# Attention with grouped queries on one core: another first ten microseconds, and one more shared chunk

## The chip, the cores and the metric

The kernel runs on one core of one Trainium2 chip. Its time is the device time of one execution in microseconds (us).

## The reference

```python
B, Hq, Hkv, Sq, Sk, D = 16, 32, 8, 288, 512, 128       # bf16
k = jnp.repeat(k, 4, axis=1); v = jnp.repeat(v, 4, axis=1)
scores = jnp.einsum("bhqd,bhkd->bhqk", q, k) * D ** -0.5
out = jnp.einsum("bhqk,bhkd->bhqd", softmax(scores), v)
```

There are 128 groups (16 x 8). A group has one K and one V of 512 rows and 4 x 288 = 1152 queries, that is nine tiles of 128.

## The kernel before

A group is three chunks of 1536 columns of scores, 384 chunks in all. TensorE computes the scores of chunk n into one of two halves of PSUM, then the values (twelve matmuls of 129 columns, the last column being the sum of the weights) of chunk n - 2. ScalarE takes the exponential of a chunk in one instruction. VectorE divides by the sums, GpSimd copies V beside its column of ones, SyncE issues the loads and stores.

```python
for n in range(NS):                  # TensorE, NS = 384
    op_s(n)                          # scores of chunk n
    if shared(n): op_sy(n)           # 120 columns of every sixth chunk go to VectorE's own exponential
    if n == 2: op_kt(1, range(NJ), 1)    # K of group 1: four transposes through PSUM
    if n >= LAG: op_pv(n - LAG)      # values, LAG = 2
```

K and the queries arrive transposed by the load, but for K of groups 0 and 1. Those come as they are, on ScalarE's queue, and TensorE transposes them. VectorE copies them out of PSUM.

```python
first = [op_q0(0), op_v(0, None, 0, 1),
         op_q(1), op_k(0, 2), op_v(0, None, 1, UG), op_q(2), op_q(3)]     # SyncE's first loads
...                                  # (lambdas left out), then, sorted by time:
sp.append((t + (2.0 if u >= NSLOT else 0.35), lambda u=u: op_v(u)))       # V of groups 4u to 4u+3
```

The first two chunks and the last go through ScalarE in three parts each, so that it can start after one matmul.

## Time and profile before

| | kernel before |
|---|---|
| time, median of the first 3 runs | 522.71 us (522.05 to 522.73) |
| span of the profiled execution | 520.0 us |
| TensorE, ScalarE, VectorE busy | 98%, 99%, 71% |
| six chunks in steady state | 7.98 us |
| first scores, first exponential | 4.41, 5.05 us |

The prediction shows the busy shares and the main groups. Two more lines of the page: the chain that ended last, by engine, and the group of the score matmuls (count, then busy time and mean ns, then idle time before them).

```profile
ACT 98%; DMA 1%; issue 1%; DVE 0%; PE 0%
...
L439 PE MATMUL ps_s<-qt_sb,kt_sb 128*128 128x512 bf16 (+2 forms) x1430 | 290.4, 320 | 5.0 <-DMA qt_sb<-in_q_dram 0.5
```

The weight loads of the same line are 1536, so 106 records of matmuls are missing from this trace: 98% for TensorE is an undercount, and the 5.0 us of idle time are mostly those holes.

### The profile page before, as it was taken

The page shows a single profiled execution, that of the slowest core. Times are in us where ns is not written, and L with a number is a line of the kernel's source. Part 1 is how long each engine was busy: PE and PEld are TensorE (multiplying, and loading weights), DVE is VectorE, ACT ScalarE, POOL GpSimd, SP SyncE. Part 2 cuts the span into 40 slices and gives each one's busy share as a digit, 9 for nine tenths or more (in the row PEclk, how much of TensorE's full clock was granted, in tenths as well). Part 3 has the DMA queues.
Part 4 walks back from the last instruction along what each step waited for, and adds up shares of the span by engine and source line. Part 5 has one row for each costly group of instructions (what it writes and reads, how often), then busy time and mean ns, then how long its engine had stood idle before and what let it go on. Part 6 is the DMA issues. An engine that isn't in the chain of part 4 may idle for free.

```text
span 520.0 us, 15243 instructions
## 1 busy us (share of the span) xinstructions
PE 510.3 (98%) x6118; PEld 394.6 (76%) x6224; DVE 369.6 (71%) x1315; ACT 513.3 (99%) x393; POOL 79.8 (15%) x135
## 2 busy tenths in 40 slices
PE   8999999999999999999999999999999999999997
PEld 5777777777777777777777777777777777777776
DVE  2767767777777677676776776767767767677776
ACT  7999999999999999999999999999999999999997
POOL 2111111111111111111111111111111111111110
PEclk9999999999999999999999999999999999999999
DMA  9999999999999998999999989999998989998212
GB/s 186 237 218 230 267 194 248 225 213 210 219 233 256 208 245 201 235 248 240 215 241 209 209 225 220 241 185 209 229 240 232 227 194 201 192 234 198 86 69 93
DMA packets 253078, 110.06 MB, mean 212 GB/s; under 512 B 219728, under 2 KB 236752, under 8 KB 253008
## 3 DMA queue, kind: packets, MB, share of 16 engines
q1 hardware_dynamic: 252720, 108.82, 97.7%
q8 instruction: 49, 0.80, 0.7%
q10 hardware_dynamic: 288, 0.26, 0.2%
q14 instruction: 21, 0.17, 0.2%
HBM read 17.04 MB, written 37.75 MB: 105 GB/s over the span
## 4 chain that ended last, share of the span: by engine, by line
ACT 98%; DMA 1%; issue 1%; DVE 0%; PE 0%
ACT pt_sb L516 97%; DMA qt_sb<-in_q_dram 1%; ACT pt_sb L511 1%; PE ps_s L439 0%; DVE o_sb L585 0%; DVE o_sb L595 0%; PE ps_s L479 0%; DVE rl_sb L575 0%; PE ps_o L669 0%; DVE bad_sb L621 0%; DVE flag_i L734 0%; DVE bad_sb L618 0%
## 5 line engine op out<-in xcount | busy, mean ns | idle before, releaser
L516 ACT ACTIVATE pt_sb<-ps_s 128x1536 bf16<-128x1536 f32 (+2 forms) x384 | 508.8, 1441 | 0.0
L479 PE MATMUL ps_o<-v_sb,pt_sb 128*128 128x129 bf16 x4584 | 322.3, 220 | 1.1
L479 PEld LDWEIGHTS ps_o<-v_sb,pt_sb 128*128 128x128 bf16 x4584 | 282.8, 98 | 49.7 <-DVE o_sb L585 14.1
L439 PE MATMUL ps_s<-qt_sb,kt_sb 128*128 128x512 bf16 (+2 forms) x1430 | 290.4, 320 | 5.0 <-DMA qt_sb<-in_q_dram 0.5
L585 DVE TENSOR_TENSOR o_sb<-ps_o,rl_sb 128x384 bf16<-128x384 f32 x382 | 211.9, 555 | 9.3 <-DVE rl_sb L575 0.5
L439 PEld LDWEIGHTS ps_s<-qt_sb,kt_sb 128*128 128x128 bf16 x1536 | 123.9, 98 | 62.3 <-issue 1.1
L575 DVE RECIPROCAL rl_sb<-ps_o 128x3 f32<-128x3 f32 x382 | 68.1, 178 | 125.5 <-PE ps_o L479 124.0
L568 POOL COPY v_sb<-vd_sb 128x512 bf16<-128x512 bf16 x128 | 78.8, 616 | 429.1 <-PE ps_o L479 408.9
L549 DVE SCALAR_TENSOR_TENSOR u_sb<-u_sb,m_sb 128x120 f32<-128x120 f32 x126 | 35.6, 283 | 2.2
L556 DVE SCALAR_TENSOR_TENSOR pt_sb<-u_sb,e_sb 128x120 bf16<-128x120 f32 x63 | 17.8, 283 | 2.2
L549 DVE SCALAR_TENSOR_TENSOR u_sb<-m_sb 128x120 f32<-128x120 f32 x63 | 17.4, 277 | 0.0
L527 DVE TENSOR_SCALAR y_sb<-ps_o 128x120 f32<-128x120 f32 x63 | 15.9, 253 | 0.0
L540 DVE TENSOR_SCALAR m_sb<-t_sb 128x120 int32<-128x120 int32 x63 | 14.1, 223 | 2.2
L540 DVE TENSOR_SCALAR e_sb<-t_sb 128x120 int32<-128x120 int32 x63 | 13.6, 216 | 0.0
L450 PE MATMUL ps_o<-qt_sb,kt_sb 128*128 128x120 bf16 x63 | 13.6, 216 | 0.0
L533 DVE TENSOR_SCALAR t_sb<-y_sb 128x120 int32<-128x120 f32 x63 | 13.4, 213 | 0.0
L450 PEld LDWEIGHTS ps_o<-qt_sb,kt_sb 128*128 128x128 bf16 x63 | 6.2, 98 | 7.4
L511 ACT ACTIVATE pt_sb<-ps_s 128x512 bf16<-128x512 f32 x6 | 3.3, 616 | 2.3 <-PE ps_s L439 2.3
L411 DVE COPY kt_sb<-ps_o 128x128 bf16<-128x128 bf16 (+2 forms) x3 | 1.0, 336 | 6.2 <-PE ps_o L404 6.1
L613 DVE TENSOR_REDUCE st_sb<-rl_sb 128x1 f32<-128x72 f32 (+1 forms) x16 | 3.5, 216 | 0.0
L611 DVE TENSOR_REDUCE st_sb<-rl_sb 128x1 f32<-128x72 f32 (+1 forms) x16 | 3.5, 216 | 0.0
L417 PE MATMUL ps_o<-const-bfloat16-1.0 128*128 128x512 bf16 (+1 forms) x6 | 2.4, 570 | 0.9 <-PEq L752 0.9
(32 smaller groups left out, 12.0 us busy)
## 6 DMA issues: line engine op xcount, KB each, us to landing
out_dram<-o_sb SPq DMA_DIRECT2D x127, 288.0 KB, 3.7
vd_sb<-in_v_dram SPq DMA_DIRECT2D x31, 512.0 KB, 5.5
qt_sb<-in_q_dram SPq DMA_TRANSPOSE x128, 4.9
kt_sb<-in_k_dram SPq DMA_TRANSPOSE x32, 5.1
vd_sb<-in_v_dram SPq DMA_DIRECT2D x1, 384.0 KB, 4.6
out_dram<-o_sb SPq DMA_DIRECT2D x3, 96.0 KB, 1.6
kd_sb<-in_k_dram ACTq DMA_DIRECT2D x2, 128.0 KB, 2.7
vd_sb<-in_v_dram SPq DMA_DIRECT2D x1, 128.0 KB, 3.3
```

The lines of the kernel that those rows point to most:

```text
L439: ins = emit(eng, w_x, lambda: eng.matmul(ps_s[:, n % 2, c:c + w], kt_sb[:, sl, j, gi, :], qg[:, t * P:t * P + w], start=True, stop=True))
L450: emit(eng, [("s_ev", n - LAG - 1)], lambda: eng.matmul(ps_o[:, (n - LAG) % 2, BANK - W:BANK], kt_sb[:, (g // UG) % NSLOT, j, g % UG, :], ...
L479: ins = emit(eng, w_x, lambda: eng.matmul(outs(r)[:, t - r % NC * TPC, :], pt(g, t, j), v_sb[:, sl, gi * NJ + j, 0:DV], start=(x == 0), st ...
L516: emit(eng, waits, lambda: eng.activation(d, s, ACTF.Exp, scale=scale)).then_inc(sem["s_e"], 1)
L527: emit(eng, [("s_yb", nth(n) - NB), ("s_pv", n - LAG + 1)], lambda: eng.tensor_scalar(out=y_sb[:, b], in0=ps_o[:, (n - LAG) % 2, BANK - W: ...
L533: emit(eng, [("s_ym", 2 * (nth(n) - NB)), ("s_y", nth(n))], lambda: eng.tensor_scalar(out=t_sb[:, b], in0=y_sb[:, b], scalar1=Y_MUL, scala ...
L540: emit(eng, [("s_yp", nth(n) - NB), ("s_yb", nth(n))], lambda: eng.tensor_scalar(out=dst[:, b], in0=t_sb[:, b], scalar1=mask, scalar2=bits ...
L549: lambda: eng.scalar_tensor_tensor(out=u_sb[:, b, x], in0=src, scalar=QUARTIC[x], in1=m, op0=ALU.add, op1=ALU.mult)
L556: lambda: eng.scalar_tensor_tensor(out=pt_sb[:, n % NPT, CH - W:CH], in0=u_sb[:, b, 2], scalar=QUARTIC[3], in1=e_sb[:, b].bitcast(FP32), o ...
L568: emit(eng, waits, lambda: eng.tensor_copy(v_sb[:, sl, gi * NJ:(gi + 1) * NJ, 0:D], vd_sb[:, sl, gi].rearrange("p (j d) -> p j d", d=D))). ...
L575: emit(eng, [("s_pv", r + 1)], lambda: eng.reciprocal(rl_sb[:, TPC * r:TPC * (r + 1)].unsqueeze(2), outs(r)[:, :, D:DV])).then_inc(sem["s_ ...
L585: emit(eng, waits, lambda: eng.tensor_tensor(out=o_sb[:, g % NO, t0:t0 + TPC, :], in0=outs(r)[:, :, 0:D], in1=rl_sb[:, TPC * r:TPC * (r + ...
```

## The change

Its intent: keep TensorE busy up to the first queries so that its clock is up, take K of group 1 off TensorE and VectorE, get the queries of group 2 sooner, let the values of chunk 1 go on before the exponential of chunk 2 is whole, and give 120 columns of one of the last chunks to VectorE. It also stores group 126 in three pieces. The core of the diff, cut:

```diff
-    FIRST = 2
-    FIRST_SHARED = 6
+    FIRST = 3
+    PARTS = {0: (1, 2, 3), 1: (2, 3), 2: (2, 3), NG * NC - 1: (1, 2, 3)}   # banks after which a part ends
+    SHARED = list(range(2 * NC, NS - NC, EVERY)) + [NS - NC]               # 6, 12, ... 378 and now 381
+    FINE = NG - 2                                                          # groups 126, 127 stored by chunk
...
-        first += [op_q(1), op_k(0, 2), op_v(0, None, 1, UG), op_q(2), op_q(3)]
+        first += [op_q(1), op_k(0, 1, 2), op_v(0, None, 1, 2), op_k(0, 2), op_q(2), op_v(0, None, 2, UG), op_q(3)]
...
-            op_warm(1, P, ps_s[:, 1])
+            op_warm(6, P, ps_s[:, 1])
...
-                if n == 2:
-                    op_kt(1, range(NJ), 1)
...
-            op_kd(eng, 1)              # ScalarE's queue: plain load of K of group 1
...
-            op_kc(1, range(NJ), 1, 3)  # VectorE: its copy
```

## The prediction

> **What bounds the kernel now.** I read the busy shares, then the chain of waits, then the timeline of the first 22 us, of a steady stretch and of the last 15 us. The busy shares and the chain come first:
>
> ```profile
> PE 510.3 (98%) x6118; PEld 394.6 (76%) x6224; DVE 369.6 (71%) x1315; ACT 513.3 (99%) x393; POOL 79.8 (15%) x135
> ...
> L516 ACT ACTIVATE pt_sb<-ps_s 128x1536 bf16<-128x1536 f32 (+2 forms) x384 | 508.8, 1441 | 0.0
> L479 PE MATMUL ps_o<-v_sb,pt_sb 128*128 128x129 bf16 x4584 | 322.3, 220 | 1.1
> ```
>
> ```profile
> 21.28 7.93 ACT pt_sb L516 x6
> 29.21 0.05 issue
> 29.26 7.93 ACT pt_sb L516 x6
> ```
>
> ScalarE's exponentials are the whole chain (98%), with no idle time booked on them, and six chunks take 7.98 us (21.28 to 29.26). But the chain names only one of two engines that are level. The starts of the exponentials in the trace lie 1.331 us apart for a full chunk, that is 1536 columns at 1.2 per ns and 51 ns. A chunk that gives 120 columns to VectorE should then take 1.231. Yet the one after it starts 128 ns over its columns' time, and the next two 67 and 55 ns, instead of 51. So of the 100 ns given away, 77 + 16 + 4 come back at once: ScalarE waits for scores. TensorE shows why. In the timeline twelve matmuls of 129 columns take 0.84 us, the last alone 0.22: 56.5 to 56.7 ns each from start to start; three of 512 columns take 0.81 with 0.379 for the last, 215.5 each. Six chunks are 72 x 56.7 + 16 x 215.5 + 8 x 56 + 3 (the split matmul of a shared chunk) = 7.98 us. That is the measured period to 0.01. **So TensorE, issuing without a gap, sets the steady rate, and ScalarE is less than 0.1 us per six chunks behind it.** A gain can only come from where TensorE stands still or runs at half rate: the first ten microseconds and the tail.
>
> ```profile
> 3.63 0.31 PE L417 MATMUL ps_s<-const-bfloat16-1.0 128*128 128x128 bf16 x1
> ...
> 4.41 2.91 PE L439 MATMUL ps_s<-qt_sb,kt_sb 128*128 128x512 bf16 x12 [0.46 <-DMA qt_sb<-in_q_dram]
> 4.81 0.15 PEld L439 LDWEIGHTS ps_s<-qt_sb,kt_sb 128*128 128x128 bf16 x1 [0.28 <-issue]
> 5.05 1.09 ACT L511 ACTIVATE pt_sb<-ps_s 128x512 bf16<-128x512 f32 x2 [2.33 <-PE ps_s L439]
> ...
> 7.30 0.23 PEld L404 LDWEIGHTS ps_o<-ident,kd_sb 128*128 128x128 bf16 x4 [0.16 <-DMA kd_sb<-in_k_dram]
> 7.31 0.40 PE L404 MATMUL ps_o<-ident,kd_sb 128*128 128x128 bf16 x4
> ...
> 7.74 0.42 DVE L411 COPY kt_sb<-ps_o 128x512 bf16<-128x512 bf16 x1 [3.51 <-PE ps_o L404]
> ...
> 8.31 0.81 PE L439 MATMUL ps_s<-qt_sb,kt_sb 128*128 128x512 bf16 x3
> ```
>
> The reader is to see: fillers end near 3.94, the first queries release TensorE at 4.41, the first exponential starts at 5.05; K of group 1 holds TensorE near 7.3, first by its load, then by four transposes, then by VectorE's copy before the scores at 8.31.
>
> **What the Trainium skill says.** "TensorE: Matmul & The Clock Gate", Part 1: the array runs at half rate until a free-running activity window of about 3.4 us was busy, so the moment of the switch varies between runs. The trace agrees: matmuls of 512 columns start at 4.41, 4.81, 5.23, 5.66 and 6.07, about 0.42 apart, then 0.215; the recorded clock goes to full at 6.04. The idle piece up to 4.41 did not prevent it in this execution. "ScalarE: Activation LUTs", What ACT_TABLE_LOAD costs: 186 ns and 0.833 ns per column, consecutive ones overlapping by about 93, so about 93 fixed. The slope agrees; the fixed part here is 51 ns, and I use that. "DMA: Bandwidth & Descriptors", Issuing engines are not separate DMA queues: loads from ScalarE and SyncE share the same 16 engines. So K of group 1 on SyncE is not more bandwidth, only another place in the order; no run here shows it yet.
>
> **The change part by part.**
>
> 1. K of group 1 by its own transposed load. It removes from TensorE the wait for the plain load (7.16 to 7.31: 0.15), four transposes (7.31 to 7.54: 0.23), and the wait for the copy (8.22 to 8.31: 0.09); from VectorE one copy of 0.42, which was not on the path. It adds one transposed load. That is issued where K of groups 2 and 3 was, at 4.21; those two groups landed after 4.1 us, at 8.3, and the queries ahead of them (2.86, 3.8 us) at 6.7. Half the data behind the same queue should land near 7.4 to 7.6. The scores of chunk 3 would want it at 7.84 (7.16 and 0.68 for the twelve value matmuls). So it just fits.
> 2. Parts: three chunks in parts instead of two, as 3, 2, 2 instead of 3, 3, 1. Seven instructions either way, so ScalarE pays nothing. The second chunk's first part now needs its second matmul, started 6.07, ended 6.45: ScalarE comes to it at 6.50, free by 0.05. The third chunk's early part lets the values of chunk 1 go on: in the trace they stop from 9.41 to 9.49, so 0.08 is saved.
> 3. Sum on TensorE: 0.15 + 0.23 + 0.09 + 0.08 = 0.55 us. But ScalarE still starts at 5.05 and runs without a gap to the end of chunk 6; the only slack there is 115 ns, the wait ahead of chunk 7 (166 ns over its columns, less 51). TensorE walks into ScalarE: the scores of chunk 5 wait for the exponential of chunk 3, which ends near 10.7 while TensorE would be there at 10.5 (0.19 given back); the late values of chunk 4 wait for the exponential of chunk 5, near 13.4 (0.14 more). That leaves TensorE at chunk 7 at about 13.6 instead of 13.76: **0.16 us**. It is kept, since from there TensorE is the bound again as soon as ScalarE has used its 0.1 per six chunks.
> 4. Fillers. Six matmuls of 128 columns at half rate, 0.107 each: from 3.63 to 4.27. They fit ahead of 4.41 and delay nothing. They gain only if the clock switches before 4.4: then the first matmul has 0.38 instead of 0.61, and 0.23 comes off the start. The switch came at 6.04 in spite of the gap, so I count 0.
> 5. Order of loads. Queries of group 2 move ahead of 256 KB of V but behind two more issues: issued near 7.5 instead of 6.2. They landed after 5.1 us, at 11.3; now near 11.8. TensorE wants them at about 12.05, ScalarE not before 12.35. Hidden, but barely.
> 6. Chunk 381 shared. ScalarE saves 100 ns there, but TensorE has the scores of 382 ready only 27 ns before ScalarE starts on them (done near 513.51, start 513.53), so at most 0.03, and I count 0.02. VectorE gets eight small instructions, 2.0 us, in the third- and fourth-last rounds. In the same pattern at chunk 378 two rounds took about 2.9 us instead of 2.66; the rounds at the end have 0.56 idle, so the reciprocal that bounds the tail (516.47) should not move.
> 7. Stores of group 126 in three pieces. The end of the program is the landing of the last store:
>
> ```profile
> SPq L227 <- DMA out_dram<-o_sb: 0.5, 1, 0.5
> ...
> SPq L223 <- DVE flag_i L734: 0.4, 1, 0.4
> ```
>
> SyncE has the flag, then waits 0.5 more for that store. Its piece is unchanged, and the transfers show idle time between the last pieces. I count 0.
>
> Sum: 0.16 + 0.02 = **0.18 us of gain**.
>
> **The rivals.** (a) A new wait replaces the old: K of group 1 or queries of group 2 land late, because the added transposed load pushes every later issue by over a microsecond. For it: transfers take 97.7% of the DMA time and landings lengthen from 3.5 to 5.4 us in this stretch. Against: K has about 0.3 us to spare, and ScalarE a further 0.6. It would cost 0.2 to 0.6, ending at 522.4 to 522.9. (b) The clock wakes earlier through the fillers: the first exponential moves up by 0.23 and TensorE wins up to 0.8 (half of 4.41 to 6.04); ScalarE then bounds for a while. For it: it is the stated intent. Against: the gap was no obstacle. It would end near 521.9. (c) ScalarE hides everything: all 0.55 is given back and nothing changes, 522.5. Against: its visible waits after shared chunks. (d) VectorE becomes the bound of the tail through chunk 381: plus 0.1 to 0.5, against it the idle 0.56.
>
> **Range and chances.** The runs before are 522.05, 522.71 and 522.73, mean 522.50; from the mean, less 0.18, **522.3 us**. Their spread of 0.7 exceeds the gain, as a switch of the clock that varies would make it. Rival (b) gives the lower side, (a) and (d) the upper: **521.6 to 522.9**. Two per cent is 10.5 us and nothing touches the steady 7.98, so within 2% has 0.994, each side 0.003.
>
> **What would show it.** Right: no transposes or VectorE copy near 7.3, scores of chunk 3 near 7.85, TensorE at chunk 7 near 13.6, the wait after chunk 6 gone or under 50 ns, 7.98 per six chunks later on, the last chunks and the wait for the last store as before. Wrong: TensorE idle on K before chunk 3 or on queries before chunk 6; a second exponential waiting for a slow matmul near 6.5, if the clock switches late; the first exponential well before 5.05; VectorE without idle time at 515.5. A loss of more than 0.5 us would mean that a late load starves TensorE further on, in groups 3 to 5, where I checked no slack.

## The result, and the profile after

| | before | after |
|---|---|---|
| median of 5 runs of the same rounds | 522.27 us (521.84 to 522.73) | 521.84 us (521.53 to 522.27) |
| ratio after to before | | 0.9992 (0.9977 to 1.0007) |
| span of the profiled execution | 520.0 us | 520.2 us |

The predicted 522.3 is 0.46 above the median, inside its range. But look at the spans: the profiled execution of the changed kernel is 0.17 us *longer*, though its median is lower. Part of that is the choice of execution: the profiled one of the kernel before took 521.67 us, less than any of its five other runs. The rest is what the experiments had to settle. The page after, busy shares, chain and score matmuls:

```profile
PE 516.2 (99%) x6226; PEld 394.6 (76%) x6226; DVE 370.5 (71%) x1322; ACT 513.4 (99%) x393; POOL 79.8 (15%) x135
...
PE 97%; DVE 2%; ACT 1%; issue 0%
...
L449 PE MATMUL ps_s<-qt_sb,kt_sb 128*128 128x512 bf16 (+2 forms) x1536 | 308.9, 324 | 0.2
```

The chain went from 98% ScalarE to 97% TensorE, with the same 7.98 us per six chunks. I don't read that as a move of the bottleneck: where two engines are level, the walk back picks one of them, and one late piece tips it. Nor is TensorE 6 us busier: this trace has all its records. The first chunks in the timeline:

```profile
3.58 0.85 PE L427 MATMUL ps_s<-const-bfloat16-1.0 128*128 128x128 bf16 x6
...
4.41 2.45 PE L449 MATMUL ps_s<-qt_sb,kt_sb 128*128 128x512 bf16 x12
4.84 1.08 ACT L521 ACTIVATE pt_sb<-ps_s 128x512 bf16<-128x512 f32 x2 [2.11 <-PE ps_s L449]
...
7.64 0.81 PE L449 MATMUL ps_s<-qt_sb,kt_sb 128*128 128x512 bf16 x3
```

The last filler starts at 4.12, so at a pace of 0.107 the fillers reach to about 4.22 (the 0.85 in the line runs to the modelled end of the last one). The first scores start at 4.41 as before, but the clock is full from 4.44, so the first exponential comes 0.21 earlier, at 4.84; the scores of chunk 3 start at 7.64 instead of 8.31. From there on ScalarE has no stop of 0.15 us or more in either kernel (the profile joins such instructions in one line). Before:

```profile
7.45 15.22 ACT L516 ACTIVATE pt_sb<-ps_s 128x512 bf16<-128x512 f32 x12
```

After:

```profile
8.57 13.89 ACT L526 ACTIVATE pt_sb<-ps_s 128x512 bf16<-128x512 f32 x11
```

Both lines end with the exponential of chunk 12, at 22.67 and 22.46: the lead is still the 0.21 of the first exponential, although the scores of chunk 3 had gained 0.67. At about the same time a quarter of a microsecond is lost (timeline, GpSimd, VectorE, weight loads; in brackets the idle time and what ended it):

```profile
22.07 1.17 POOL L578 COPY v_sb<-vd_sb 128x512 bf16<-128x512 bf16 x2 [7.68 <-DMA vd_sb<-in_v_dram]
...
22.46 0.30 DVE L543 TENSOR_SCALAR t_sb<-y_sb 128x120 int32<-128x120 f32 x1
22.80 0.52 DVE L550 TENSOR_SCALAR m_sb<-t_sb 128x120 int32<-128x120 int32 x1
...
25.11 0.68 PEld L489 LDWEIGHTS ps_o<-v_sb,pt_sb 128*128 128x128 bf16 x12 [0.60 <-DVE o_sb L595]
```

V of groups 4 to 7 came late, so GpSimd copies for two groups run back to back, 22.07 to 23.24. Two of VectorE's small instructions of chunk 18, 0.21 and 0.22 long elsewhere, take 0.30 and 0.52: they end at 22.76 and 23.32, each 75 ns after the end of a copy. The divisions behind them are late, TensorE stands for 0.27 us, and the exponential of chunk 16 starts 1.59 after that of 15 instead of 1.33. The Trainium skill, "SBUF — State Buffer", Who interferes with whom, says that VectorE's second pair of ports is also GpSimd's, and that an instruction which has it keeps it to its end while one of the other engine that needs it is blocked. The traces agree: 0.52 against 0.22 here, and in e1 a 0.21 became 0.65 and again ended 75 ns after a copy. An instruction of the same kind that reads PSUM kept its 0.25 beside a copy (e11).

I read the starts of the exponentials from both traces and added up the lead of the execution after, in us (minus is faster): first exponential -0.21; from there to chunk 7, and to chunk 15, 0.00; chunk 15 to 16 +0.26; 16 to 381 +0.04; 381 to the last exponential +0.05; from there to the end +0.03. The sum is +0.17, the difference of the spans.

### The profile page after: what moved, and what is told of

The parts are those of the page before. It is cut to its first block, busy times and chain, and to the rows that moved or that the text cites. A ratio compares the mean times of both kernels' runs of the same rounds, so it can differ in the third digit from the quotient of the medians.

```text
span 520.2 us, 15366 instructions
## 1 busy us (share of the span) xinstructions
PE 516.2 (99%) x6226; PEld 394.6 (76%) x6226; DVE 370.5 (71%) x1322; ACT 513.4 (99%) x393; POOL 79.8 (15%) x135
## 4 chain that ended last, share of the span: by engine, by line
PE 97%; DVE 2%; ACT 1%; issue 0%
PE ps_o L489 49%; PE ps_s L449 46%; PE ps_o L460 1%; ACT pt_sb L521 1%; ACT pt_sb L526 1%; PE ps_o L427 0%; DVE o_sb L595 0%; DVE u_sb L559 0%; DVE rl_sb L585 0%; DVE m_sb L550 0%; PE ps_s L427 0%; DVE pt_sb L566 0%; PE ps_o L414 0%; DVE t_sb L543 0%; DVE o_sb L605 0%
## 5 line engine op out<-in xcount | busy, mean ns | idle before, releaser
L449 PE MATMUL ps_s<-qt_sb,kt_sb 128*128 128x512 bf16 (+2 forms) x1536 | 308.9, 324 | 0.2
L543 DVE TENSOR_SCALAR t_sb<-y_sb 128x120 int32<-128x120 f32 x64 | 13.7, 214 | 0.0
L521 ACT ACTIVATE pt_sb<-ps_s 128x512 bf16<-128x512 f32 (+1 forms) x6 | 4.3, 748 | 2.1 <-PE ps_s L449 2.1
```

The costliest lines, as they stand in the source:

```text
L449: ins = emit(eng, w_x, lambda: eng.matmul(ps_s[:, n % 2, c:c + w], kt_sb[:, sl, j, gi, :], qg[:, t * P:t * P + w], start=True, stop=True))
L543: emit(eng, [("s_ym", 2 * (nth(n) - NB)), ("s_y", nth(n))], lambda: eng.tensor_scalar(out=t_sb[:, b], in0=y_sb[:, b], scalar1=Y_MUL, scala ...
```

## The experiments

Twelve runs followed: nine other kernels, and the two of the comparison again. The table has the moment of the clock switch, the start of the first exponential, and differences of starts of exponentials, all from the trace of one execution of each (us). "Last exp." is the last of the three parts of chunk 383, and "end" the start of the last record, 0.05 before the span ends:

| run | switch | first exp. | first to chunk 7 | 15 to 16 | 381 to last exp. | last exp. to end |
|---|---|---|---|---|---|---|
| before | 6.04 | 5.05 | 9.557 | 1.331 | 3.617 | 4.11 |
| e2 before | 6.43 | 5.09 | **10.540** | 1.330 | 3.614 | 4.10 |
| e8 before, six fillers | 5.59 | 4.93 | 9.676 | 1.331 | 3.617 | 4.00 |
| e5 before, own load of K | 5.59 | 4.95 | 9.559 | 1.330 | 3.613 | 4.54 |
| after | 4.44 | 4.84 | 9.559 | **1.591** | 3.665 | 4.14 |
| e1 after | 4.47 | 4.97 | 9.559 | **1.641** | 3.666 | 4.16 |
| e11 after | 6.60 | 5.06 | **9.795** | 1.330 | 3.663 | 4.02 |
| e3 after, one filler | 4.72 | 4.98 | 9.558 | 1.330 | 3.665 | 4.18 |
| e4 after, V earlier | 4.90 | 5.07 | 9.567 | 1.331 | 3.667 | 4.17 |
| e6 after, 381 whole | 4.64 | 4.87 | 9.559 | 1.330 | 3.615 | 4.00 |
| e9 e6, queries split | none recorded | 5.50 | 9.559 | 1.330 | 3.613 | 3.99 |
| e10 e6, V earlier | 6.31 | 5.05 | 9.655 | 1.330 | 3.614 | 4.00 |
| e12 e10, parts as before | 6.71 | 4.96 | 9.557 | 1.331 | 3.616 | 4.01 |

From chunk 16 to 381 all of them take 485.60 to 485.65, so the change moves the middle by 0.04 at most. The three traces of the kernel before all have 485.60, all others 0.02 to 0.04 more; I didn't look for the cause. e7 is not in the table, as it changes the middle on purpose. e2, e3 and e8 are single runs.

### The same two kernels again (e1, e2, e11)

No edit.

> The changed kernel once more, unaltered. Theory A (the moment of the clock switch is the free-running window's, not the fillers'): the switch falls at another time than 4.44 us, anywhere from about 4.3 to 7.7; if it falls after 4.8, the first exponential is at about 5.05 again and the exponential of chunk 7 starts at about 14.6, as in the kernel before. Rival B (the fillers bring the switch forward): switch near 4.44 again, first exponential near 4.84, chunk 7 near 14.40. In both, the collision near 22 to 25 us (two copies of V on GpSimd on top of VectorE's chain of chunk 18, TensorE idle 0.27 us) should come again, as it follows from the order of the loads. Time 521.5 to 522.3.

> The kernel before once more, for a second sample of its clock switch. Theory A: a switch at another time than 6.04 us. If it is before 4.4: first exponential at 4.84, but chunk 7 at 14.5 or later, because K of group 1 holds TensorE at 7.3 whatever the clock. Rival B: the switch again near 6.04. No double copy of V inside VectorE's chain of chunk 18; the wait before chunk 16 under 60 ns.

> The changed kernel unaltered, on the same chip as the two above, for a fair comparison and a third look at where V of groups 4 to 7 lands. Theory: from chunk 381's start to the start of the last exponential 3.665 again; chunk 7 starts 9.56 us after the first exponential again; if the copy for group 4 starts later than 21.5 us, 1.6 us from chunk 15 to 16, else 1.33. Median 0 to 0.5 below the kernel before, 0.2 to 0.4 above the kernel with chunk 381 whole.

e1: 521.94 us (521.70 to 522.04; before 522.01, 521.81 to 523.00, ratio 0.9993, 0.9979 to 1.0006). e11: 521.94 (521.70 to 522.31; before 522.25, 522.00 to 522.80, ratio 0.9993). e2: one run, 522.68. In e1 the switch was near 4.44 again, as the rival had it, and the collision came again (V issued at 17.1, landed after 4.8). In e11 the switch was at 6.60, so the rival fell. V was issued at 15.9 and the copies began at 21.53 and 22.22: no loss, although I had set the limit at 21.5. A second expectation failed there: chunk 7 came 9.795 after the first exponential, not 9.56 (see e12).

e2 was the surprise. The kernel before has a slow draw that its first trace did not show. Timeline of e2, weight loads, matmuls, ScalarE:

```profile
8.46 0.23 PEld L404 LDWEIGHTS ps_o<-ident,kd_sb 128*128 128x128 bf16 x4 [1.10 <-DMA kd_sb<-in_k_dram]
8.46 0.40 PE L404 MATMUL ps_o<-ident,kd_sb 128*128 128x128 bf16 x4 [0.93 <-DMA kd_sb<-in_k_dram]
...
9.47 0.81 PE L439 MATMUL ps_s<-qt_sb,kt_sb 128*128 128x512 bf16 x3
...
10.31 1.45 ACT L516 ACTIVATE pt_sb<-ps_s 128x1536 bf16<-128x1536 f32 x1 [0.83 <-PE ps_s L439]
```

The plain load of K of group 1, issued at 4.30 on ScalarE's queue, landed after 4.1 us; in the first trace it took 3.0, in e8 3.3. TensorE stood on it until 8.46, the scores of chunk 3 came at 9.47 instead of 8.31, ScalarE stood for 0.83, and everything after is 0.98 us late (10.540 instead of 9.557). K's own load landed after 2.9 to 3.7 us in the eleven traces that have it, so the late landing was not seen again; why it came in e2 is open.

### The fillers (e3, e8)

e3: the changed kernel with one filler. e8: the kernel before with six.

```diff
-            op_warm(6, P, ps_s[:, 1])
+            op_warm(1, P, ps_s[:, 1])        # e3; the reverse in e8
```

> The changed kernel with one filler instead of six ahead of the first queries. Theory A: a switch at a time that bears no relation to the filler, 4.3 to 7.7. Rival B: always later than 5, near 6.04 as in the kernel before.

> The kernel before with six fillers instead of one ahead of the first queries, nothing else. Theory A (free-running window): the clock switches at any time between about 3.3 and 6.7 us. Rival B (the fillers bring it forward): 4.4 to 4.9, as in the three runs of the changed kernel with fillers. In both, if K of group 1 lands near 7.3, chunk 7 starts no earlier than 14.5.

One filler: switch at 4.72 (time 521.74, one run). Six fillers in the kernel before: 5.59 (521.57, one run). Over all traces, six fillers had 4.44, 4.47, 4.64, 4.73 (e7), 4.90, 5.59, 6.31, 6.60 and 6.71, and one filler 4.72, 5.59, 6.04 and 6.43. The fillers do not decide it; the profiled pair was a lucky draw. The time at full clock is 515.41 us in all of these but e7, whatever the kernel's length, and 522.24 in the longer e7. The difference is 6.83, or two windows of the 3.413 us that the Trainium skill gives ("TensorE: Matmul & The Clock Gate", Part 1), as a free-running window would have it, that is one that does not start with the kernel. e8 also shows what binds the start when K is a little late: the first exponential was 0.12 earlier than in the first trace, and chunk 7 started at 14.60 all the same, as K of group 1 landed at 7.4. Thirteen executions cannot exclude a small effect on the odds.

### K of group 1 alone (e5)

```diff
-first += [op_q(1), op_k(0, 2), ...]
+first += [op_q(1), op_k(0, 1, 2), op_k(0, 2), ...]
...                                   # and op_kt(1), op_kc(1), op_kd(1) removed
```

> The kernel before with one part of the change alone: K of group 1 by its own transposed load, the rest and the order of the other loads as before. Theory C (the kernel before has two modes: the plain load of K of group 1 lands at 7.3 us in one execution and at 8.46 in another, and the late one costs 1.0 us): the late mode, 522.7 to 523.0, goes; K lands by 7.6. But the queries of group 2 are now issued one transposed load later, behind 384 KB of V, and should land near 12.5 to 13; TensorE wants them at 12.35, so a new stop of 0.2 to 0.7 us before chunk 6. Median 521.9 to 522.5, highest 522.6. Rival: the late mode of the kernel before comes from something else (the clock), and this kernel shows 522.7 to 523.0 as often.

522.15 us (522.01 to 522.56; before 521.86, 521.41 to 522.45, ratio 1.0008, 0.9994 to 1.0021). Chunk 7 comes 9.559 after the first exponential, so this part alone does what the whole change does there. The stop that I expected for the queries of group 2 did not come in the trace, so their move is not shown to be needed. No run was above 522.6, but on that chip the kernel before had no slow draw either, in nine runs. So the times do not show that the own load cures the slow draw; only the traces do. Why this kernel's median is 0.3 higher is open: in its trace the end is 0.43 longer than in the first trace of the kernel before, through a last store that was issued 0.30 late and took 1.9 us to land, against 1.7. I have no cause for that.

### Chunk 381 (e6)

```diff
-    SHARED = list(range(2 * NC, NS - NC, EVERY)) + [NS - NC]
+    SHARED = list(range(2 * NC, NS - NC, EVERY))
```

> The changed kernel with chunk 381 whole. Theory: sharing it gained nothing, as TensorE's scores of 382 come no earlier; from the start of chunk 381 to the start of the last exponential 3.617 us, as in the kernel before, against 3.665 in the changed kernel; and 0 to 0.08 shorter from there to the end of the program. Rival (the prediction): 0.02 us longer without the sharing, 3.63 to 3.69. Time within 0.2 of the changed kernel.

521.40 us (521.24 to 521.75; before 521.86, ratio 0.9992, 0.9978 to 1.0006). 3.615 as the theory had it: sharing the chunk costs 0.05 up to the last exponential, in all five traces of the table that share it against the eight that do not. The matmul of the 120 columns waits 0.04 for VectorE's division, which puts the scores of 382 back. After that, of the kernels that store group 126 in pieces, those with the chunk shared need 4.02 to 4.18 to the end (five traces), those with it whole 3.99 to 4.01 (four). VectorE's last rounds show how (timeline of VectorE, after, then e6):

```profile
514.57 0.60 DVE L559 SCALAR_TENSOR_TENSOR u_sb<-u_sb,m_sb 128x120 f32<-128x120 f32 x2
515.20 0.28 DVE L566 SCALAR_TENSOR_TENSOR pt_sb<-u_sb,e_sb 128x120 bf16<-128x120 f32 x1
515.40 0.55 DVE L595 TENSOR_TENSOR o_sb<-ps_o,rl_sb 128x384 bf16<-128x384 f32 x1
515.87 0.17 DVE L585 RECIPROCAL rl_sb<-ps_o 128x3 f32<-128x3 f32 x1
516.08 0.56 DVE L595 TENSOR_TENSOR o_sb<-ps_o,rl_sb 128x384 bf16<-128x384 f32 x1
```

```profile
514.26 0.56 DVE L595 TENSOR_TENSOR o_sb<-ps_o,rl_sb 128x384 bf16<-128x384 f32 x1
515.38 0.18 DVE L585 RECIPROCAL rl_sb<-ps_o 128x3 f32<-128x3 f32 x1 [0.56 <-PE ps_o L489]
515.59 0.56 DVE L595 TENSOR_TENSOR o_sb<-ps_o,rl_sb 128x384 bf16<-128x384 f32 x1
```

With the chunk whole VectorE still idles 0.56 there; with it shared the idle time is gone, the division of chunk 381 ends at 516.63, and the store of that chunk is issued at 517.04 (516.55 in e6), right on top of the last two. That the bunched stores make the end longer is my reading, not shown by itself.

### No chunk shared at all (e7)

```diff
-    SHARED = list(range(2 * NC, NS - NC, EVERY)) + [NS - NC]
+    SHARED = []
```

> The changed kernel with no chunk shared: ScalarE does all columns. Theory D (TensorE sets the steady rate, ScalarE is 0.1 us per six chunks behind it): six chunks take 6 x 1.331 = 7.986 us instead of 7.981, about 0.3 us more in all: 522.0 to 522.6. Rival (ScalarE is the bound, as the chain of waits of the kernel before has it with 98%): 64 x 0.100 = 6.4 us more, 528.

526.93 us (526.65 to 527.49; before 521.86, ratio 1.0099, 1.0083 to 1.0114). Both expectations fell: 5.1 us more, neither 0.3 nor 6.4. Six chunks take 8.06 us (chunk 100 at 139.41, chunk 300 at 408.07), not 7.986. In 200 us of steady state TensorE now waits 2.04 us ahead of value matmuls, 0.08 per six chunks; with sharing, in the kernel before, no value matmul inside a chunk's twelve starts there more than 57 ns after the one ahead of it, and 57 is the pace. ScalarE waits too: its starts are 66 to 70 ns over the columns' time in two chunks of three, against 51 when it waits for nothing. So here two engines that feed each other and are level both lose: each waits a little for the other. The 100 ns per shared chunk are what lets TensorE run without a gap. So the sharing in the middle is worth 0.08 per six chunks, and TensorE is the bound *because* of it.

### V of groups 4 to 7 earlier (e4, e10)

```diff
-            sp.append((t + (2.0 if u >= NSLOT else 0.35), lambda u=u: op_v(u)))
+            sp.append((t + (2.0 if u >= NSLOT else 0.1), lambda u=u: op_v(u)))
```

> The changed kernel with V of groups 4 to 7 issued ahead of the queries of group 4 instead of after them (near 14.5 instead of 17.1 us). Theory: V lands near 19.5, the copy for group 4 runs alone near 19.5 and that for group 5 near 22, VectorE's chain of chunk 18 is not held, TensorE's 0.27 us stop near 24.9 is gone, and the start of chunk 16 relative to chunk 15 is back from 1.59 to 1.33 us: 0.26 us faster than the changed kernel in a run of the same clock switch, so near 521.6. Rival: the stop is not from the copies, and stays.

> The changed kernel with chunk 381 whole and V of groups 4 to 7 ahead of the queries of group 4. Theory: no double copy inside VectorE's chain of chunk 18, chunk 16 starts 1.33 us after chunk 15 in every draw; 0.3 less than the changed kernel in those executions in which it collides. Rival (seen in the times of the earlier run with that order, 521.88 to 522.68): the queries of group 4 land too late in some executions and cost as much as is won: times spread over 0.6 or more and the median no lower than with chunk 381 whole alone.

e4: 522.23 us (521.88 to 522.68; before 522.01, ratio 1.0001, 0.9987 to 1.0014). e10, with chunk 381 whole: 521.61 (521.58 to 521.85; before 522.25, ratio 0.9986, 0.9973 to 1.0000), 0.33 below the changed kernel of the same rounds (e11). In both traces the copies lie apart (19.34 and 22.00; 18.96 and 22.07) and the collision is gone. By itself that proves little, as four of the six traces with V later have no collision either; the cause is shown by the instructions of after and e1 that end 75 ns after a copy. But e4's times are no better: its median is 0.29 above that of the changed kernel of the same rounds (e1), and the next run shows why an earlier V is a gamble.

### The parts as before (e12)

```diff
-    FIRST = 3
-    PARTS = {0: (1, 2, 3), 1: (2, 3), 2: (2, 3), NG * NC - 1: (1, 2, 3)}
+    FIRST = 2
+    PARTS = {0: (1, 2, 3), 1: (1, 2, 3), NG * NC - 1: (1, 2, 3)}
...                                   # on top of e10
```

> The changed kernel with three of its parts undone or altered: chunk 381 whole, V of groups 4 to 7 ahead of the queries of group 4, and the parts of the first chunks as in the kernel before (three, three, one). What stays of the change: K of group 1 by its own load, the order of the first loads, the fillers, the stores. Theory: chunk 7 starts 9.56 us after the first exponential whatever the moment of the clock switch (the merged first part of chunk 1 cost 0.10 and 0.24 us where the switch came at 6.31 and 6.60); chunk 16 starts 1.33 after chunk 15; 3.615 from chunk 381 to the last exponential. Median 0.3 to 0.7 below the kernel before on the same chip, and a narrow spread of 0.4 or less. Rival: the parts of chunk 2 were needed, now that K does not hold TensorE, and chunk 7 comes later than 9.56.

522.04 us (521.63 to 522.68; before 522.20, 521.86 to 523.11, ratio 0.9997, 0.9983 to 1.0011). The first half of the theory holds: with the latest switch of all, 6.71, chunk 7 comes 9.557 after the first exponential. With the changed kernel's parts a late switch cost 0.10 (e10, 6.31) and 0.24 (e11, 6.60). ScalarE in e11, the merged part in the second line:

```profile
6.03 0.60 ACT L526 ACTIVATE pt_sb<-ps_s 128x512 bf16<-128x512 f32 x1
6.76 1.02 ACT L521 ACTIVATE pt_sb<-ps_s 128x1024 bf16<-128x1024 f32 x1
```

The second starts 0.73 after the first, where 0.48 is the pace of a part that waits for nothing: it waits for a fifth matmul at half clock. Neither the narrow spread came nor the gain of 0.3 to 0.7: the medians are 0.16 apart. In the trace of e12 the queries of group 4, now behind V, are late (timeline, TensorE and ScalarE):

```profile
20.85 0.77 PE L449 MATMUL ps_s<-qt_sb,kt_sb 128*128 128x512 bf16 x3 [0.37 <-DMA qt_sb<-in_q_dram]
...
21.66 1.35 ACT L526 ACTIVATE pt_sb<-ps_s 128x1416 bf16<-128x1416 f32 x1 [0.32 <-PE ps_s L449]
```

They were issued at 14.66 and landed after 6.1 us, at 20.8; TensorE had wanted them at 20.3 (0.53 us stand between its matmuls there), and from chunk 7 to 15 this execution takes 11.21 us where all others take 10.66 or 10.67. In e10 they took 5.5 from 14.32 and just made it.

### The first queries in two pieces (e9)

```diff
-first = [op_q0(0), op_v(0, None, 0, 1)]
+first = [op_q0(0), op_q0(1)]          # tiles 0 to 3, tiles 4 to 8; V of group 0 on ScalarE's queue
...                                   # on top of e6
```

> The changed kernel without the sharing of chunk 381, and with the first group's queries loaded in two pieces (four tiles, then five), V of group 0 moved to ScalarE's queue. From what the runs showed: everything up to chunk 7 hangs on the first exponential (chunk 7 starts 9.56 us after it), and that hangs on the first queries at 4.3 to 4.4 us. Less than half the data should land near 3.6; then the copies of K of group 0 (done at 4.24) and the slow clock hold the scores, and the first exponential comes at 4.3 to 4.6 instead of 4.84 to 5.05. K of group 1 is issued 0.6 us later and lands near 8.1, where the scores of chunk 3 want it by about 7.8: some 0.3 given back. Gain 0.2 to 0.5 against the kernel with chunk 381 whole: near 521.1. Rival: the landing time is nearly the same for half the data (a fixed cost), and the first exponential stays at 4.85 to 5.05; then 521.4 or more.

522.25 us (522.02 to 523.49; before 522.25, ratio 1.0004, 0.9990 to 1.0017). A miss, beyond the rival: four tiles of nine released the first scores at 5.08 instead of 4.3 to 4.4, with the second piece and V behind them. The first exponential came at 5.50 and chunk 7 again 9.559 after it. Half the data did not land sooner in this order; whether the second piece or V held it is open.

## Why the prediction was right or wrong

The time fell in the range, and no gain clear of noise was forecast or found. That says little for the steps: the range is 1.3 us wide, and rival (c), no gain at all, lies in it too. By its own steps:

- **TensorE sets the steady rate: right**, by the missing gaps, but "ScalarE is less than 0.1 us per six chunks behind it" hid how much hangs on that little: without it 5.1 us (e7).
- **Step 1, K of group 1: right in what it removes, wrong in what that is worth.** I sized it by one execution, in which K landed at 7.3. There it was worth nothing. e2 has K landing at 8.4, and there it costs 0.98. Over the three sets of rounds in which the changed kernel ran, its 15 runs have a median of 521.94 and none above 522.31. The kernel before has 522.13 in 23 runs, of which seven lie at 522.7 to 523.0 and the other sixteen have a median of 522.02. So against the ordinary draw the change gains at most 0.1; the rest is the slow draws that are gone. That these are all late K is likely, but one trace shows it.
- **Step 3, the failed step: "That leaves TensorE at chunk 7 at about 13.6 instead of 13.76: 0.16 us."** The gain there is 0.00. ScalarE runs from the first exponential to that of chunk 5 without a stop in both kernels: the latter starts 6.876 us after the former before and 6.874 after. The last four value matmuls of chunk 4 wait for its end (a pause of 83 ns before and 117 after, where 57 is the pace), and the scores of chunk 7 start 0.29 us after it. That holds in every trace but e2 and e8, where K came late. So the kernel before already stood at the wait that I counted as new, and of the 0.55 us on TensorE all is given back, as rival (c) had it. The slip: I let the exponential of chunk 5 end near 13.4, by its pace of 1.33. The record before has it start at 11.925 and last 1.542, to 13.47, and 0.29 more is the 13.76 of the kernel before. The step's sum doesn't close either: 0.55 less 0.19 less 0.14 is 0.22, not 0.16, and ScalarE's slack of 115 ns is less than both. In eight of thirteen traces, of both kernels, chunk 7 starts 9.56 us after the first exponential, and never sooner. TensorE's 13.55 at chunk 7 in the profiled execution is near the predicted 13.6 by luck: it is the 0.21 of the clock switch at 4.44.
- **Step 2: right, with the risk named**: it was worked out as free by 0.05 for a switch at 6.04, which no run of the changed kernel had; 0.10 and 0.24 were lost at 6.31 and 6.60. The 0.08 for the values of chunk 1 went into the same waiting.
- **Step 4, fillers count 0: right**; rival (b) looked right in the first trace and fell in e3, e8 and e11.
- **Step 5: the queries of group 2 landed near 11.8 as worked out** (issued at 7.49, 4.3 to landing). But I followed the later issues only that far. The load of V for groups 4 to 7 was issued at 13.7 to 14.8 in the three traces of the kernel before and at 15.4 to 17.1 in the six of the table with the changed order, and in two of those six it ran into VectorE (0.26 and 0.31). The prediction named "groups 3 to 5, where I checked no slack": that was the place.
- **Step 6, chunk 381: wrong in sign.** I counted 0.02 of gain; it costs 0.05 up to the last exponential, and likely another 0.1 after. Rival (d) was right about the engine: VectorE's idle 0.56 was used up.
- **Step 7, stores: 0, not contradicted**: with chunk 381 whole, 3.99 to 4.01 from the last exponential to the end with three pieces (four traces), and 4.00, 4.10, 4.11 and 4.54 with one. No run changes the stores alone, so a gain of 0.1 is not excluded.

What stays: K off the ScalarE queue is probably worth having, for the slow draw alone. Chunk 381 is better whole, by the traces. e6 and e10 have the lowest medians against the kernel before of the same rounds, by 0.46 and 0.64, but no interval separates them from the changed kernel (0.9992 and 0.9986 against 0.9992 to 0.9993), and the order of e10 can lose 0.5 in a bad draw.

## What to carry to other kernels

When two engines are level, ask what each waits for in every draw, not in one trace: a load that was just in time in the profiled execution may be a microsecond late in the next. Before a stop on one engine is counted as gain, look in the trace whether the next wait for the other engine already binds in the unchanged kernel. Work out an end by the recorded duration of an instruction, not by the pace of a pipelined row. And a load that moves to the front moves every later one back: follow the queue until a stage with slack, and look at which two engines will then copy and compute at the same moment.

## What the Trainium skill lacked or had wrong

- "TensorE: Matmul & The Clock Gate": it gives a sustained busy window as the condition for full clock, without saying how busy. In e3 the clock rose at 4.72, and the window of 3.41 us up to there held a stretch of about 0.7 us, from 3.72 to 4.42, in which TensorE had no matmul. In the first trace of the kernel before it rose at 6.04, so the window ahead ended at 2.63 (6.04 less 3.41); that one was idle up to 0.86, as far as the trace goes, and the clock did not rise.
- "ScalarE: Activation LUTs": about 93 ns fixed per instruction in a row, an estimate from its figures (186 less an overlap of 93); 51 here for 1536 columns from PSUM (1.331 us from start to start).
- "DMA: Bandwidth & Descriptors": it gives a bandwidth for transposed loads, but no time from issue to landing while other loads run. Over all traces here the issue alone took 1.2 to 5.2 us and landing 2.9 to 9.1, and the same load in the same place of the order took 0.7 longer in e12 than in e10.
- No page has what two level engines lose to each other in a loop: 0.08 us per six chunks in e7, where the sums of either alone give 7.98 and 7.99 and the loop takes 8.06.
